# A kernel planner's transfer model: queue, engines and landing by kind, and transposes that hold the queue

## The chip, the cores and the metric

The kernel runs on one core of one Trainium2 chip. The metric is the device time of one execution in microseconds (us). Three runs of the kernel before took 1390.72 (the median), 1385.05 and 1391.09 us. The profiled execution took 1391.44 us; its instructions span 1389.6 us, and the remaining 1.84 us lie around them.

## The reference

For each of 8 sequences of 3136 rows and 256 channels, the input `x` is filtered in the frequency domain and then goes through a mixing block with a two-layer perceptron:

```python
X = np.fft.rfft(x, axis=1)
y = np.fft.irfft(X * (filt_r + 1j * filt_i), n=3136, axis=1)      # filter along the sequence
u = y + np.real(np.fft.fft(np.fft.fft(y, axis=1), axis=2))        # mix rows and channels
un = (u - mean(u)) / np.sqrt(var(u) + 1e-6)                       # over the channels
out = u + np.maximum(un @ w_ch1, 0.0) @ w_ch2                     # 256 -> 1024 -> 256
```

## The kernel before, in words

**The stages.** Each Fourier transform is split in two stages of small matrix products, with a regrouping through DRAM between them. For one sequence `b` the way is:

- `load_x` (L590) loads seven tiles of x, 480 KB each for b of 2 and over (448 KB for the first two). `measure_x` (L600) squares them on ACT, and `weigh_x` turns the result into a scale; a small PE transpose in `pow2` (L470) is its first PE step.
- `first_pair` (L671) is the first forward stage. Its results go to DRAM (`d1`, L695) and come back regrouped (`load_at`, L801).
- `spectrum` (L890) is the second forward stage. DVE (L909) and POOL (L925, L927) apply the filter, ACT and POOL (L952, L954) split the result into two fp16 halves, and a DMA transpose (L958) writes it to `z`. There are 14 of these transposes for a sequence, two for each of 7 chunks.
- `inverse1` (L1066, L1075) multiplies a chunk of `z`, and its result goes to DRAM (`d2`, L1112). `load_b2` (L1138) brings it back regrouped.
- `inverse2` (L1198) finishes the filter; `bring` (L1235) writes rows to DRAM (`dy`). `fetch` (L1264) reads them back in groups of 256.

The 8 sequences give 49 groups `g` of 256 rows, each row two tokens. `prepare` mixes channels (L1305, L1330, L1355) and normalizes; `normalize` makes `un` (L1507), splits it (L1529, L1535) and transposes it with a DMA (L1538) into `ut`; groups 0 and 6 are transposed on PE instead (L1515). `products` then runs 392 steps, eight for a group: six matmuls of the first layer (`h`, L1564), ACT and DVE split their rectified result (L1591, L1593), and twice six matmuls add the second layer (`acc`, L1604). `finish` (L1618) adds the input, and `store` (L1624) writes the result.

**What sets the order.** Every engine runs its instructions in the order in which they were emitted, and waits in place for what the next one needs. That order is made before the kernel runs, by a small planner: `Plan` (from L63 on) is an event simulation written in Python. Each stage above is a generator. It yields an engine, a length in microseconds and, if wanted, a priority; the planner lets each engine, as it comes free in planned time, take the waiting task of the lowest priority number, and only then is the task's instruction emitted. A task that needs an event (`until`), a buffer (`take`) or a step of `products` (`gate`) does not stand in line before it has come, again in planned time. The stages of a sequence are tied to the steps of `products` by such gates, so that they spread evenly among the 392 steps.

All DMAs are issued on one queue, SP's. For it the planner keeps `moved`, the planned time at which all transfers so far have been moved. A transfer that takes the queue at `now` is planned so (in `Plan.run`):

```python
issue = TURN if length == 1.65 else ISSUE
self.moved = max(self.moved, self.now + issue + REACH) + length
self.free_at[e] = max(self.now + issue, self.moved - BACKLOG)
self.end = self.moved + LANDED
```

with ISSUE 0.5, TURN 1.4, REACH 0.5, BACKLOG 4.5 and LANDED 1.5; the length 1.65 marks a DMA transpose. So the queue is taken for `issue` or until no more than 4.5 us of transfers are ahead, and the task goes on at `end`. Tasks in the line "calm" also go to SP, but only when `moved` is at most CALM (1.0) ahead.

The planner never sees the chip: where a transfer lands later than planned, an engine meets an instruction whose data are not there and waits, with everything that was emitted behind it.

Of the kernel before, what the change touches and what calls it, by code (L numbers as in the profile page):

```python
# [42 lines left out]
PASSES = ((0, 0), (1, 0), (0, 1))  # L43
BACKED = 6.5
RAW_IN = (None, None, "ys", "ys", "ut", None, None, None)
ISSUE = 0.5
TURN = 1.4
BACKLOG = 4.5
REACH = 0.5
LANDED = 1.5  # L50
HOP = 0.1
SMALL = 2.0**-20
CALM = 1.0
# [12 lines left out]
class Plan:  # L66


    def __init__(self):
        self.now = self.end = self.moved = 0.0  # L70
        self.heap, self.count, self.live = [], 0, 0
        self.queues = {e: [] for e in ("PE", "DVE", "ACT", "POOL", "SP", "calm")}
        self.free_at = dict.fromkeys(self.queues, 0.0)
# [72 lines left out]
    def given(self, ring, k):  # L146
        ring.freed.add(k)
        self.grant(ring)

    def run(self):  # L150
        while self.heap:
            self.now, _, f, args = heapq.heappop(self.heap)
            f(*args)
            while self.heap and self.heap[0][0] <= self.now:
                _, _, f, args = heapq.heappop(self.heap)
                f(*args)
            for e, queue in self.queues.items():
                if e == "calm" and queue:
                    e = "SP"
                    if self.moved > self.now + CALM:  # L160
                        self.post(self.moved - CALM, int)
                        continue
                if queue and self.free_at[e] <= self.now:
                    _, _, task, length = heapq.heappop(queue)
                    if e == "SP":
                        issue = TURN if length == 1.65 else ISSUE
                        self.moved = max(self.moved, self.now + issue + REACH) + length
                        self.free_at[e] = max(self.now + issue, self.moved - BACKLOG)
                        self.end = self.moved + LANDED
                    else:  # L170
                        self.end = self.free_at[e] = self.now + length
                    self.post(self.free_at[e], int)
                    self.step(task, None, self.free_at[e] if e == "SP" else None)
        assert not self.live
# [199 lines left out]
def _program(ctx, tc, nc, a, NB):  # L374
# [205 lines left out]
    def load_x(b, t):  # L580
        yield gate(t)
        ms[b] = tp.tile([len_of(b), 8], F32, tag="mx", name=f"mx_{b}")
        for q in range(7):
            yield gate(t + 1.2 * q)
            yield until(("own", "x", b, q))
            if b == 1:
                yield until(("asked_b2",))
            yield "calm" if b == 2 else "SP", 1.6, -62 if b == 1 else t + 1.2 * q
            src = a["x"][b] if b < WIDE else a["xq"][b - WIDE]
            nc.sync.dma_start(xs[b, q], src[:, 4 * q : 4 * q + 4])  # L590
            done("x", b, q)
# [65 lines left out]
    def first_pair(b, q, t):  # L657

        yield gate(t)
        yield until(("sx", b), ("s1q",))  # L660
        if b not in d1s:
            d1s[b] = dp.tile([2, 56, 28, 2, 256], F16, tag="d1", name=f"d1_{b}")
        x = xs[b, q]
        sx = sxs[b][:, 1:2]
        kp = yield take("psf", 2)
        ps = [bank(f"s1_{b}_{q}_{i}").rearrange("p (n c) -> p n c", n=2) for i in range(2)]
        yield "PE", FOURS, t - BOOST
        for c in range(2):
            for i in range(2):
                row = slice(64 * i, 64 * i + 56)  # L670
                nc.tensor.matmul(  # L671
                    ps[i][64 * c : 64 * c + 64], s1q[row], x[row, 2 * c : 2 * c + 2], start=True, stop=True
                )
        give("big", 21 * b + q - 7)
        kx = yield take("x16")
        odd = fp.tile([128, 2, 256], F32, tag="x16", name=f"odd_{b}_{q}", bufs=3)
        yield "ACT", 0.58
        nc.scalar.activation(odd, ps[1], AF.Copy, scale=sx)
        for out, op in ((ps[1], ALU.subtract), (odd, ALU.add)):
            yield "DVE", 0.73  # L680
            nc.vector.scalar_tensor_tensor(out, ps[0], sx, odd, op0=ALU.mult, op1=op)
        give("psf", kp)
        k = yield take("ast")
        st = fp.tile([128, 2, 2, 2, 256], F16, tag="ast", name=f"ast_{b}_{q}", bufs=3)
        yield "ACT", 0.55
        nc.scalar.copy(st[:, 1, :, 0], ps[1])
        plan.spawn(sum_half(b, q, kx, odd, st), t)
        yield "DVE", 0.66
        nc.vector.tensor_tensor(st[:, 1, :, 1], ps[1], st[:, 1, :, 0], op=ALU.subtract)
        give("psf", kp + 1)  # L690
        yield until(("sum", b, q))
        for c in range(2):
            yield "SP", 0.85
            n = 4 * q + 2 * c
            nc.sync.dma_start(  # L695
                d1s[b][:, :, n : n + 2].rearrange("s p n h c -> p s (n h c)"),
                st[64 * c : 64 * c + 56].rearrange("p s n h c -> p s (n h c)"),
            )
        give("ast", k)
        done("d1", b, 2 * q)  # L700
        done("d1", b, 2 * q + 1)
# [68 lines left out]
    turned = []  # L770
# [14 lines left out]
    def load_at(b, t):  # L785
        yield until(*(("d1", b, q) for q in range(14)))
        if b < WIDE:
            d1v = d1s[b].rearrange("(u r) n h c -> (r n h) u c", r=2)
        else:
            d1v = d1s[b].rearrange("s (j r) n h c -> (r n h) s j c", r=2)  # L790
        for ch in range(7):
            yield gate(t + max(0, ch - 2))
            yield until(("own", "at", b, ch))
            if b < WIDE:
                yield "SP", 1.95, t + max(0, ch - 2)
                nc.sync.dma_start(ats[b, ch], d1v[:, 8 * ch : 8 * ch + 8])
            else:
                at = ats[b, ch].rearrange("p (j s) c -> p s j c", s=2)
                for i in range(2):
                    yield "SP", 1.0, t + max(0, ch - 2)  # L800
                    nc.sync.dma_start(at[:, i], d1v[:, i, 4 * ch : 4 * ch + 4])  # L801
            done("at", b, ch)

# [51 lines left out]
    def spectrum(b, ch, hf, t):  # L855
# [98 lines left out]
        nc.gpsimd.tensor_tensor(y16v[:, 1], yh, y16v[:, 0], op=ALU.subtract)  # L954
        done("ylo", b, ch, hf)
        yield until(("own", "z", b, ch))
        yield "SP", 1.65
        nc.sync.dma_start_transpose(  # L958
            zs[b, ch][:, :, 128 * hf : 128 * hf + 128], y16.rearrange("p l j q -> p (l j q)")
        )  # L960
# [93 lines left out]
    def inverse1(b, ch, t):  # L1054
# [52 lines left out]
        else:  # L1107
            yield until(("low", b, ch))
        for c in range(2):
            yield "SP", 0.65  # L1110
            j = 4 * ch + 2 * c
            nc.sync.dma_start(d2s[b][:, j : j + 2], bt[64 * c : 64 * c + 56])  # L1112
        give("ast", k)
# [12 lines left out]
    def load_b2(b):  # L1126
        yield until(*((("d2", b, ch) if b else ("d2", 0, ch, h)) for ch in range(7) for h in range(1 if b else 2)))
        if b:
            d2v = d2s[b].rearrange("(i a r) j l t c -> i (r j) a (l t c)", a=2, r=2)
        else:  # L1130
            d2v = d2s[b].rearrange("(i a r) j t c -> i (r j) a (t c)", a=2, r=2)
        for c in range(7):
            yield gate(brought(b, c) - 3 - (0 if b else 3))
            k = yield take("b2")
            b2 = b2_page(k, b)
            for o in range(2):
                yield "SP", 1.0, urgent(b, c) - 3 if b or c > 1 else -63
                nc.sync.dma_start(b2[64 * o : 64 * o + 56].rearrange("p a l t c -> p a (l t c)"), d2v[2 * c + o])  # L1138
            if b == 0 and c == 1:
                plan.set(ev("asked_b2"), True)  # L1140
            b2s[b, c] = k, b2
            done("b2", b, c)
# [74 lines left out]
    def bring(b, c, o, ys, ky, kp, p):  # L1217
# [13 lines left out]
            return  # L1231
        rows = dys[b][224 * c : 224 * c + 224].rearrange("(j q) k c -> k q j c", j=4)
        for h in range(2):
            yield "SP", 0.7 - 0.17 * (c == 0)
            nc.sync.dma_start(rows[h, :, c == 0 :], ys[64 * h : 64 * h + 56, c == 0 :])  # L1235
            for kind in range(2 * (c == 0)):
                yield "SP", 0.1
                nc.sync.dma_start(
                    rows[kind, 28 * h : 28 * h + 28, 0], ys[64 * h + 28 * kind : 64 * h + 28 * kind + 28, 0]
                )  # L1240
# [7 lines left out]
    def fetch(g):  # L1248
# [7 lines left out]
        for t in range(2):  # L1256
            q, g1 = 256 * g + 128 * t, 256 * g + 128 * t + 128
            yield until(*(("placed", b, o // 2, o % 2) for b, o in pieces(q, g1, 112)))
            while q < g1:
                b = q // NS  # L1260
                e = min(g1, (b + 1) * NS)
                p = q % 128
                yield "SP", 1.6 * (e - q) / 256
                nc.sync.dma_start(y[p : p + e - q, t], dys[b][q - b * NS : e - b * NS])  # L1264
                q = e
            if t:
# [234 lines left out]
    def normalize(g, t, y, sb, ut):  # L1501
# [32 lines left out]
            yield "POOL", 1.14  # L1534
            nc.gpsimd.tensor_tensor(u16[:, :, :, 1], unv, u16[:, :, :, 0], op=ALU.subtract)  # L1535
        give("un", ku)
        yield "SP", 1.65
        nc.sync.dma_start_transpose(ut[:, t], u16.rearrange("p k d l q -> p (k d l q)"))  # L1538
        give("u16", k6)
        done("ut", g, t)  # L1540
# [79 lines left out]
        plan.spawn(store(g, t, y), 8 * g + 8)  # L1620

    def store(g, t, y):
        yield "SP", 0.8
        nc.sync.dma_start(a["out"][256 * g + 128 * t : 256 * g + 128 * t + 128], y[:, t])  # L1624
        outs[g] = outs.get(g, 0) + 1
        if outs[g] == 2:
# [250 lines left out]
```

## Time and profile before

| | |
|---|---|
| time, median of 3 runs | 1390.72 us |
| profiled execution | 1391.44 us |
| its span | 1389.6 us |
| PE busy | 1354.4 us, 97% of the span |
| DVE, ACT, POOL busy | 72%, 61%, 51% |
| mean granted TensorE clock | 0.992 of full speed |
| DMA engines, mean busy share by the queue's packets | 77.8% |
| HBM read and written | 113.72 MB and 99.09 MB |
| DMA transposes | 98 into `z`, 94 into `ut` |

PE is TensorE's matmul row. An engine that is busy 97% of the time has little idle time to lose, so the table is read together with the list of what PE waited for, and with the granted clock where PE had been idle. In the views of waits, "A <- B" is an engine's instruction and what released it. In the queue's rows, SPq is SP's queue, and the second number is how long the issue held it, not how long the transfer took.

### The profile page before, as it was taken

The page shows a single profiled execution, that of the slowest core. Times are in us where ns is not written, and L with a number is a line of the kernel's source. Part 1 is how long each engine was busy: PE and PEld are TensorE (multiplying, and loading weights), DVE is VectorE, ACT ScalarE, POOL GpSimd, SP SyncE. Part 2 cuts the span into 40 slices and gives each one's busy share as a digit, 9 for nine tenths or more (in the row PEclk, how much of TensorE's full clock was granted, in tenths as well). Part 3 has the DMA queues.
Part 4 walks back from the last instruction along what each step waited for, and adds up shares of the span by engine and source line. Part 5 has one row for each costly group of instructions (what it writes and reads, how often), then busy time and mean ns, then how long its engine had stood idle before and what let it go on. Part 6 is the DMA issues. An engine that isn't in the chain of part 4 may idle for free.

```text
span 1389.6 us, 33404 instructions
## 1 busy us (share of the span) xinstructions
PE 1354.4 (97%) x12879; PEld 917.6 (66%) x12879; DVE 997.1 (72%) x2162; ACT 845.3 (61%) x1631; POOL 706.4 (51%) x865
## 2 busy tenths in 40 slices
PE   9989999999899999999999999999899999999998
PEld 8845766666657765677656665666566776666666
DVE  6888896788678777678677875777648778465442
ACT  6776567556755677565765667647656565444341
POOL 2713881378536864388443863368614766222210
PEclk9989999999999999999999999999999999999999
DMA  9797998699889897887979797787966986554320
GB/s 259 238 249 209 240 202 208 204 227 205 195 231 238 184 199 192 256 188 185 228 197 217 174 218 182 216 205 170 221 176 180 205 197 168 141 138 105 100 61 31
DMA packets 353603, 265.35 MB, mean 191 GB/s; under 512 B 216188, under 2 KB 290588, under 8 KB 353444
## 3 DMA queue, kind: packets, MB, share of 16 engines
q1 hardware_dynamic: 353444, 263.22, 77.8%
q8 instruction: 101, 1.65, 0.5%
q14 instruction: 58, 0.48, 0.1%
HBM read 113.72 MB, written 99.09 MB: 153 GB/s over the span
## 4 chain that ended last, share of the span: by engine, by line
PE 72%; DMA 8%; DVE 7%; POOL 4%; ACT 4%; issue 3%; SPq 2%; DVEq 0%; POOLq 0%; ACTq 0%
PE acc L1604 29%; PE h L1564 29%; DMA x<-xq 4%; PE s L671 3%; PE y L1198 3%; PE s L890 2%; PE mix L1305 2%; PE i L1075 2%; DMA z<-late 1%; DMA ft<-fiT 1%; ACT xsq L600 1%; DVE h L1593 1%; DMA ft<-frT 1%; POOL eo L1011 1%; POOL late L954 1%
## 5 line engine op out<-in xcount | busy, mean ns | idle before, releaser
L1604 PE MATMUL acc<-w2s,h 128*128 128x256 f16 x4704 | 589.0, 273 | 1.2 <-ACT u L1529 1.0
L1564 PE MATMUL h<-ut,w1s 128*128 128x512 f16 x2352 | 575.6, 381 | 0.2 <-DVE ut L1521 0.2
L1604 PEld LDWEIGHTS <-h 128*128 128x128 f16 x4704 | 449.1, 98 | 138.9 <-issue 24.2
L1593 DVE SCALAR_TENSOR_TENSOR h<-h,h 128x512 f16<-128x512 f32 x392 | 267.8, 683 | 227.1 <-ACT h L1591 225.3
L1591 ACT ACTIVATE h<-h 128x512 f16<-128x512 f32 x392 | 232.8, 594 | 305.6 <-PE h L1564 303.6
L1564 PEld LDWEIGHTS <-w1s 128*128 128x128 f16 x2352 | 225.8, 98 | 205.9 <-issue 14.2
L1535 POOL TENSOR_TENSOR u<-un,u 128x512 f16<-128x512 f32 x92 | 106.4, 1157 | 222.5 <-ACT u L1529 186.5
L1355 POOL TENSOR_TENSOR pages<-sm,pages 128x508 f32<-128x508 f32 x49 | 62.0, 1266 | 107.0 <-ACT sm L1396 66.0
L1507 ACT ACTIVATE un<-pages,sb 128x256 f32<-128x256 f32 x196 | 109.0, 592 | 10.0 <-DVE sb L1454 8.9
L954 POOL TENSOR_TENSOR late<-yt,late 128x448 f16<-128x448 f32 x98 | 102.7, 1052 | 21.2 <-ACT late L952 19.8
L707 POOL TENSOR_TENSOR ast<-odd,ast 128x512 f16<-128x512 f32 x42 | 48.4, 1157 | 123.6 <-ACT ast L705 118.7
L1476 DVE BATCH_NORM_STATS2 st<-pages 128x6 f32<-128x256 f32 x196 | 80.6, 411 | 12.9 <-POOL pages L1361 11.2
L1330 DVE SCALAR_TENSOR_TENSOR pages<-mix,alpha,pages 128x254 f32<-128x254 f32 (+2 forms) x184 | 81.4, 476 | 9.0 <-ACT sm L1396 7.5
L909 DVE SCALAR_TENSOR_TENSOR yt<-s,pF,ft 128x448 f32<-128x448 f32 x98 | 66.0, 674 | 28.1 <-PE s L890 27.0
L1120 POOL TENSOR_TENSOR bt<-sd,bt 128x512 f16<-128x512 f32 x42 | 48.6, 1158 | 70.3 <-ACT bt L1118 70.0
L925 POOL TENSOR_TENSOR yt<-yt,t 128x224 f32<-128x224 f32 x98 | 64.6, 659 | 36.1 <-DVE t L909 33.7
L952 ACT CAST late<-yt 128x448 f16<-128x448 f32 x98 | 54.9, 562 | 40.0 <-POOL yt L927 39.5
L1224 ACT ACTIVATE ys<-y,alpha 128x512 f32<-128x512 f32 x98 | 62.2, 682 | 26.3 <-PE y L1198 22.3
L1618 DVE SCALAR_TENSOR_TENSOR pages<-acc,beta,pages 128x512 f32<-128x512 f32 x98 | 68.6, 741 | 7.3 <-PE acc L1604 7.2
L978 POOL TENSOR_TENSOR ef<-yt 128x224 f32<-128x224 f32 x112 | 72.6, 669 | 0.3
L1011 POOL TENSOR_TENSOR eo<-ef,eo 128x448 f16<-128x448 f32 (+6 forms) x62 | 59.7, 967 | 25.2 <-ACT eo L1007 16.9
L909 DVE SCALAR_TENSOR_TENSOR t<-s,pF,ft 128x448 f32<-128x448 f32 x98 | 65.9, 673 | 0.5 <-POOL yt L927 0.5
(191 smaller groups left out, 1676.6 us busy)
## 6 DMA issues: line engine op xcount, KB each, us to landing
pages<-d SPq DMA_DIRECT2D x112, 224.0 KB
out<-pages SPq DMA_DIRECT2D x98, 256.0 KB
pages<-dy SPq DMA_DIRECT2D x90, 256.0 KB
d<-ast SPq DMA_DIRECT2D x98, 224.0 KB
d<-bt SPq DMA_DIRECT2D x98, 224.0 KB
dy<-ys SPq DMA_DIRECT2D x96, 224.0 KB
x<-xq SPq DMA_DIRECT2D x42, 480.0 KB
at<-d SPq DMA_DIRECT2D x84, 224.0 KB
```

The costliest lines, as they stand in the source:

```text
L909: nc.vector.scalar_tensor_tensor(out, p, pF[:, 1:2], f, op0=ALU.mult, op1=ALU.mult)
L954: nc.gpsimd.tensor_tensor(y16v[:, 1], yh, y16v[:, 0], op=ALU.subtract)
L978: nc.gpsimd.tensor_tensor(eft[:, i], yt[:, 0, i], yt[:, 1, i], op=o)
L1011: nc.gpsimd.tensor_tensor(lo, efv[:, :, e0 : e0 + n], hi, op=ALU.subtract)
L1330: nc.vector.scalar_tensor_tensor(out, p, al, y, op0=ALU.mult, op1=ALU.add)
L1476: nc.vector.bn_stats(st[:, 2 * t + k], y[:, t, k])
L1507: nc.scalar.activation(un[:, k], y[:, t, k], AF.Identity, bias=sb[:, i, 1:2], scale=sb[:, i, 3:4])
L1535: nc.gpsimd.tensor_tensor(u16[:, :, :, 1], unv, u16[:, :, :, 0], op=ALU.subtract)
L1564: nc.tensor.matmul(p.rearrange("p (t k q) -> p t k q", t=2, k=2), w1s[:, d, hw, 128 * f : 128 * f + 128], utv[:, :, :, d, hx], start=i == ...
L1591: nc.scalar.activation(h[:, 0], p, AF.Relu)
L1593: nc.vector.scalar_tensor_tensor(h[:, 1], p, 0.0, h[:, 0], op0=ALU.max, op1=ALU.subtract)
L1604: nc.tensor.matmul(acc[:, kind], h[:, hh, c0 : c0 + 128], w2s[:, f, hw], start=f == 0 and kind == 0 and i == 0, stop=f == 7 and kind == 1 ...
```

## The change

It changes the planner alone. No instruction is added to the kernel or taken from it; what can change is the order on each engine's queue. The transfer rule becomes a method of its own. A transpose (length TURN, now 1.42) takes the queue for 1.3 instead of 1.4, its data start to move after 1.1 instead of 1.9, and it holds the queue until 0.3 before the transpose ahead of it has been moved. Any other transfer starts to move after 1.6 instead of 1.0, and the queue may run ahead further: 6.0 us before this transfer is counted, instead of 4.5 after it is. A transfer is planned to have landed 0.7 after it was moved, instead of 1.5.

```diff
-ISSUE = 0.5
-TURN = 1.4
+ISSUE = 0.48
+TURN = 1.42
 BACKLOG = 4.5
-REACH = 0.5
-LANDED = 1.5
+LANDED = 0.7
...
+    def transfer(self, length):
+        turned = length == TURN
+        issue, reach, room = (1.3, 1.1, BACKLOG) if turned else (ISSUE, 1.6, BACKLOG + 1.5)
+        free = max(self.now + issue, self.moved - room)
+        self.moved = max(self.moved, self.now + reach) + length
+        if turned:
+            free = max(free, self.turned - 0.3)
+            self.turned = self.moved
+        self.free_at["SP"] = free
+        self.end = self.moved + LANDED
...
                     if e == "SP":
-                        issue = TURN if length == 1.65 else ISSUE
-                        self.moved = max(self.moved, self.now + issue + REACH) + length
-                        self.free_at[e] = max(self.now + issue, self.moved - BACKLOG)
-                        self.end = self.moved + LANDED
+                        self.transfer(length)
```

The lengths of the kinds become:

| transfer | before | after |
|---|---|---|
| tile of x (L590) | 1.6 | 2.0 |
| `d1`, half a tile (L695) | 0.85 | 0.83 |
| `at` (L801), whole and half | 1.95, 1.0 | 1.75, 0.87 |
| DMA transposes (L958, L1538) | 1.65 | 1.42 |
| `d2` (L1112) | 0.65 | 0.95 |
| `b2` (L1138) | 1.0 | 0.88 |
| `dy` (L1235) | 0.7 | 0.74 |
| `fetch`, 256 rows (L1264) | 1.6 | 1.92 |
| `store` (L1624) | 0.8 | 0.61 |

## Rows read from the trace of the kernel before

**Rows 1.** The page's first part: busy time of each engine.

```profile
PE 1354.4 (97%) x12879; PEld 917.6 (66%) x12879; DVE 997.1 (72%) x2162; ACT 845.3 (61%) x1631; POOL 706.4 (51%) x865
```

**Rows 2.** Windows: stretch, its length, busy time of PE, PEld, DVE, ACT, POOL; clock; DMA.

```profile
0.00:94.00 94.00, 82.29 (x607) 69.58 (x608) 74.86 (x157) 70.16 (x145) 37.09 (x50) 0.97 0.89 249
...
140.00:1389.60 1249.60, 1226.63 (x11987) 823.33 (x11985) 885.72 (x1914) 744.03 (x1428) 658.05 (x801) 1.00 0.78 186
```

**Rows 3.** What PE waited for from 140 us on: total, times, longest.

```profile
PE i L1075 <- DMA z<-late: 7.7, 3, 6.4
PE pt_x L470 <- ACT mx L617: 6.5, 4, 2.8
...
PE acc L1604 <- ACT u L1529: 1.0, 1, 1.0
```

**Rows 4.** The queue in time, 986 to 1003 us: start, time held, line, transfer, count.

```profile
986.77 0.35 SPq L1264 DMA_DIRECT2D pages<-dy  x1
987.22 1.30 SPq L1112 DMA_DIRECT2D d<-bt  x2
988.57 2.15 SPq L590 DMA_DIRECT2D x<-xq  x3
990.82 0.41 SPq L1264 DMA_DIRECT2D pages<-dy  x1
991.27 0.71 SPq L590 DMA_DIRECT2D x<-xq  x1
992.09 3.93 SPq L958 DMA_TRANSPOSE z<-late  x1
996.13 2.15 SPq L1112 DMA_DIRECT2D d<-bt  x2
998.37 4.28 SPq L958 DMA_TRANSPOSE z<-late  x1
```

**Rows 5.** PE in time, 1000 to 1016 us; in brackets the idle time before.

```profile
1000.45 1.46 PE L1564 MATMUL h<-ut,w1s 128*128 128x512 f16 x6
1008.28 1.49 PE L1075 MATMUL i<-z,late 56*64 56x256 f16 x24 [6.38 <-DMA z<-late]
1009.71 2.74 PE L1604 MATMUL acc<-w2s,h 128*128 128x256 f16 x12
1012.25 2.17 PE L1564 MATMUL h<-ut,w1s 128*128 128x512 f16 x6
1014.25 1.47 PE L1604 MATMUL acc<-w2s,h 128*128 128x256 f16 x12
```

**Rows 6.** PE in time, 844 to 862 us.

```profile
844.95 0.85 PE L1075 MATMUL i<-z,late 56*64 56x256 f16 x24 [0.48 <-DMA z<-late]
...
856.54 0.26 PE L470 MATMUL pt_x<-ident,mx 120*1 120x120 f32 x1 [2.82 <-ACT mx L617]
856.64 2.72 PE L1604 MATMUL acc<-w2s,h 128*128 128x256 f16 x12
859.16 1.92 PE L1564 MATMUL h<-ut,w1s 128*128 128x512 f16 x6
```

**Rows 7.** Windows, columns as in rows 2, over two stretches of lower clock.

```profile
856.67:860.08 3.41, 3.41 (x16) 2.05 (x15) 1.88 (x8) 3.38 (x7) 2.04 (x2) 0.50 0.29 70
1006.85:1013.68 6.83, 5.40 (x40) 3.32 (x41) 0.87 (x3) 1.15 (x2) 1.08 (x3) 0.50 1.12 262
```

**Rows 8.** Time that an issue held the queue, by line: ns least/median/most.

```profile
L958 SPq DMA_TRANSPOSE z<-late x98: 1231/1363/6704, 149.7 to 1162.2; - x98
```

**Rows 9.** The same for an ordinary transfer of 224 KB.

```profile
L1112 SPq DMA_DIRECT2D d<-bt x98: 306/379/1508, 168.4 to 1182.7; - x98
```

**Rows 10.** The queue in time, 348 to 365 us.

```profile
348.34 4.72 SPq L590 DMA_DIRECT2D x<-xq  x6
353.17 11.35 SPq L958 DMA_TRANSPOSE z<-late  x2
```

**Rows 11.** The chain that ended last, 465 to 490 us: start, us from issue to landing.

```profile
472.94 3.10 DMA z<-late
```

More of the change, by code (lines that the diff above doesn't have):

```diff
@@ L69, in __init__ @@
     def __init__(self):
-        self.now = self.end = self.moved = 0.0
+        self.now = self.end = self.moved = self.turned = 0.0
         self.heap, self.count, self.live = [], 0, 0
@@ L587, in load_x @@
                 yield until(("asked_b2",))
-            yield "calm" if b == 2 else "SP", 1.6, -62 if b == 1 else t + 1.2 * q
+            yield "calm" if b == 2 else "SP", 2.0, -62 if b == 1 else t + 1.2 * q
             src = a["x"][b] if b < WIDE else a["xq"][b - WIDE]
@@ L692, in first_pair @@
         for c in range(2):
-            yield "SP", 0.85
+            yield "SP", 0.83
             n = 4 * q + 2 * c
@@ L794, in load_at @@
             if b < WIDE:
-                yield "SP", 1.95, t + max(0, ch - 2)
+                yield "SP", 1.75, t + max(0, ch - 2)
                 nc.sync.dma_start(ats[b, ch], d1v[:, 8 * ch : 8 * ch + 8])
@@ L799, in load_at @@
                 for i in range(2):
-                    yield "SP", 1.0, t + max(0, ch - 2)
+                    yield "SP", 0.87, t + max(0, ch - 2)
                     nc.sync.dma_start(at[:, i], d1v[:, i, 4 * ch : 4 * ch + 4])
@@ L956, in spectrum @@
         yield until(("own", "z", b, ch))
-        yield "SP", 1.65
+        yield "SP", TURN
         nc.sync.dma_start_transpose(
@@ L1109, in inverse1 @@
         for c in range(2):
-            yield "SP", 0.65
+            yield "SP", 0.95
             j = 4 * ch + 2 * c
@@ L1136, in load_b2 @@
             for o in range(2):
-                yield "SP", 1.0, urgent(b, c) - 3 if b or c > 1 else -63
+                yield "SP", 0.88, urgent(b, c) - 3 if b or c > 1 else -63
                 nc.sync.dma_start(b2[64 * o : 64 * o + 56].rearrange("p a l t c -> p a (l t c)"), d2v[2 * c + o])
@@ L1233, in bring @@
         for h in range(2):
-            yield "SP", 0.7 - 0.17 * (c == 0)
+            yield "SP", 0.74 - 0.17 * (c == 0)
             nc.sync.dma_start(rows[h, :, c == 0 :], ys[64 * h : 64 * h + 56, c == 0 :])
@@ L1262, in fetch @@
                 p = q % 128
-                yield "SP", 1.6 * (e - q) / 256
+                yield "SP", 1.92 * (e - q) / 256
                 nc.sync.dma_start(y[p : p + e - q, t], dys[b][q - b * NS : e - b * NS])
@@ L1536, in normalize @@
         give("un", ku)
-        yield "SP", 1.65
+        yield "SP", TURN
         nc.sync.dma_start_transpose(ut[:, t], u16.rearrange("p k d l q -> p (k d l q)"))
@@ L1622, in store @@
     def store(g, t, y):
-        yield "SP", 0.8
+        yield "SP", 0.61
         nc.sync.dma_start(a["out"][256 * g + 128 * t : 256 * g + 128 * t + 128], y[:, t])
```

## The prediction

> **What bounds the kernel now.** I read the busy times first. PE is busy for 1354.4 us of the span [rows 1], so the change can only win what lies between that and 1389.6 us, 35.2 us, and what PE loses at a lower clock. The windows say where the 35.2 us lie: 94 less 82.3, or 11.7 us, before products start, 23.0 us from 140 us on, the wait for the last store among them, and the small rest between [rows 2]. The waits of PE say why: from 140 us on, 7.7 us in 3 waits for transposes into `z`, 6.5 us in 4 waits of `pt_x` (the scale of a new sequence, which hangs on its last x tile through ACT), and one of 1.0 us [rows 3]. All other reasons together are small.
>
> The queue's own rows show what the two large kinds have in common. At 988.57 us x tiles are issued, four with one `fetch` between them; behind them a transpose holds the queue for 3.93 us, and after two ordinary stores the next one holds it for 4.28 us [rows 4]. PE comes to the `inverse1` that needs this second transpose and stands idle for 6.38 us, until 1008.28 [rows 5]. At 348.34 six x tiles are issued in a row, and the two transposes behind them hold the queue for 11.35 us [rows 10]. So the waits sit where x tiles and transposes meet, a few times in the run.
>
> The idle time is paid for twice. After it the granted clock is 0.50, the lower level of 1.2 GHz, for 6.83 us from 1006.85 on and for 3.41 us from 856.67 on [rows 7]. In the first, `i` takes 1.49 us where 0.85 is usual [rows 5, 6], `acc` 2.74 instead of 1.47 and `h` 2.17 instead of 1.46 [rows 5]: 0.64 + 1.27 + 0.71 = 2.6 us. In the second `acc` takes 2.72 and `h` 1.92 [rows 6]: 1.25 + 0.46 = 1.7 us.
>
> **The change part by part.** No instruction is added or removed, so PE's 1354.4 us of work stay. What moves is the order. It matters only where PE meets an instruction too early.
>
> *Transposes behind x tiles.* I put the old and the new rule, by hand, on the measured issue times from 986.77 us on [rows 4]. Old: the `fetch` is moved at 986.77 + 1.0 + 1.6 = 989.37, two `d2` at 990.67, three x tiles at 992.27, 993.87 and 995.47, `fetch` at 997.07, x at 998.67, the transpose at 1000.32, two `d2` at 1001.62, the second transpose at 1003.27; with 1.5 for landing it is there at 1004.8. PE got it at 1008.28 [rows 5], so the old plan is 3.5 us early. New: 986.77 + 1.6 + 1.92 = 990.29, then 992.19, 998.19, 1000.11, 1002.11, 1003.53, 1005.43, 1006.85, and with 0.7 it lands at 1007.55, 0.7 us early. The hold comes out right as well: the old rule holds the queue for 1.4 us at the second transpose, the new one until 1003.53 - 0.3 = 1003.23, so 4.9 us, and 4.28 us was measured [rows 4]. For the first one the new rule says until 1002.11 - 4.5 = 997.61, that is 5.5 us against 3.93.
>
> A planner that knows this gives PE other work, as products wait for nothing there: the next instructions, `acc` and `h`, run at once after the wait [rows 5]. The error falls from 3.5 to 0.7 us, by 80%; I take 75%, since the other places are not this one. What the late transposes and x tiles cost PE is 7.7 + 6.5 + 1.0 [rows 3] + 2.6 + 1.7 of lower clock = 19.5 us. Three quarters of it are a gain of 14.6 us; the ends are 19.5 (all) and half, 9.7.
>
> A transpose holds the queue for at least 1.231 us and at most 6.704 [rows 8], where an ordinary transfer holds it for 0.306 to 1.508 us [rows 9]; a hold that long only a transpose has. The Trainium skill (Advanced Engine Details and Errata, section on the X-bar transpose) says instead that transpose DMAs are as fast as regular ones. By that rule there would be no hold to plan for, and of the correction only the longer x tiles would stay, 4 x 0.4 = 1.6 of 3.5 us; the trace here does not agree.
>
> *Landings that are planned earlier.* A transpose alone was planned to land after 1.4 + 0.5 + 1.65 + 1.5 = 5.05 us, and now after 1.1 + 1.42 + 0.7 = 3.22 us; one took 3.10 us [rows 11]. So the plan is right, but 1.83 us of cover are gone, and in a full queue the landing of every kind comes 0.8 us earlier. Of 49 `inverse1` only 3 waited for `z` [rows 3], because gates hold most of them back far longer. The exposed ones are the last two chunks of the seven sequences after the first, 14 in all, as x tiles of the next sequence come among them. The two small waits for `z` were 7.7 - 6.38 = 1.32 us together, 0.66 each. From below this part costs nothing, as for the 46 without a wait; from above 14 x 0.66 = 9.2 us. I take 0.3 each, 4.2 us, between the two, since the gates cover part of them.
>
> *Other lengths.* `at`, `b2`, `d1` and stores become shorter by 0.02 to 0.20 us, `d2`, `dy` and `fetch` longer by 0.04 to 0.32. No PE wait after 140 us names `at`, so I cost them at nothing; their cover is the same gates, and without it they are of the size of the 0.66 above.
>
> *The start.* Before 94 us the new lengths reorder loads among each other. PE is idle for 11.7 us there [rows 2]; I take no change and keep 3 us, a quarter of it, both ways.
>
> **Sum**, against the profiled execution of 1391.4 us (0.7 above the median of 1390.7): 1391.4 - 14.6 + 4.2 = 1381.0 us, 0.7% under the median.
>
> **The rivals.** *The wait moves on (1387).* An x tile needs the buffer that an `inverse1` of the sequence before gives back. If that is planned later, the last x tile and `pt_x` come later too, and the 6.5 us of `pt_x` with their 1.7 us of lower clock stay in one form or another. Then the gain is three quarters of 7.7 + 1.0 + 2.6 = 11.3, so 8.5, and 1391.4 - 8.5 + 4.2 = 1387. For it speaks that the x tiles' burst itself stays, against it that products have work to put there. By the rule of the skill above it would be 46% of 19.5, 9.0 us, and about 1387 too; the trace leaves that 2 in 100. This rival, with changes that do nothing to the order at the places that matter (1391), has 0.30.
>
> *No slack left (1402).* The plan is now so tight that `inverse1` sits on PE right at the planned landing. If each of the 14 exposed ones loses the whole 1.83 us, they cost 25.6 us: 1391.4 - 14.6 + 25.6 = 1402. It decides from new waits of about 21 us on, 1.5 us each. For it speaks that a transpose's landing spreads (holds from 1.2 to 6.7 us [rows 8]), against it the 46 that wait for nothing. The Trainium skill (DMA: Bandwidth & Descriptors, section on latency and other measured facts) gives 0.2 us for an access to HBM on average and 2 us at high load, which speaks for late landings just where the plan now cuts 0.8 us; the place worked out above, among x tiles, shows the new rule 0.7 us early, so a part of that is there. Chance 0.12.
>
> **How the numbers follow.** The forecast with what surrounds it, a gain of over 0.5% (below 1383.8), has 0.58. Half a per cent is about what a measurement of this kernel can tell from no change. Within it lie the moved wait and the change without effect, 0.30; slower by more is the rival without slack, 0.12. The range: from all 19.5 us gained, no new waits and 3 us at the start, 1391.4 - 19.5 - 3 = 1369, to half of the gain, 9.2 us of new waits and 3 us lost at the start, 1391.4 - 9.7 + 9.2 + 3 = 1394. What lies outside is the rest of the slower rival and surprises at the start, together under 2 in 10.
>
> **What would show it.** Right: PE's waits for `z` and for `pt_x` from 140 us on shrink from 14.2 us to under 5, the long one of 6.38 us is gone, the clock stays at its upper level from 140 us to the end, and PE's busy time falls a little (the 4.3 us at the lower clock). The holds of the queue by transposes stay as long as they are, since only the plan of them changes. Wrong: if the waits for `pt_x` stay with the `z` waits gone, the wait has moved on; if PE waits a dozen times for 1 to 2 us for `z`, `at` or `b2`, the slack was worth more than the truth; if PE's idle time before 94 us changes by over 3 us, the start decided, which this sum leaves out.

## The result, and the profile after

The changed kernel takes 1404.2 us (median of 6 runs, 1401.2 to 1409.7) against 1390.7 (6 runs, 1385.1 to 1392.8): a ratio of 1.0115, interval 1.0093 to 1.0136. (The ratios here and below are estimated over all runs and differ a little from the quotient of the two medians, which is 1.0097 here.) It is slower, by 13.5 us. The profiled execution took 1409.7 us, the longest of the six, and its span is 1407.9; what the profiles account for below is therefore 18.3 us and not 13.5. Lines of the changed kernel from the planner's loop on are 7 higher than before: `inverse1` is L1082 for L1075, the first layer L1571 for L1564.

The page's first part after, answering to [rows 1]:

```profile
PE 1360.8 (97%) x12879; PEld 919.2 (65%) x12879; DVE 1003.0 (71%) x2162; ACT 846.7 (60%) x1631; POOL 707.7 (50%) x865
```

The same 12879 matmuls take 6.4 us longer, and the span is 18.3 us longer, so 11.9 us are new idle time. The windows, columns as in [rows 2], say where:

```profile
0.00:94.00 94.00, 81.11 (x601) 69.12 (x601) 72.04 (x151) 65.85 (x135) 37.75 (x50) 0.96 0.86 240
94.00:140.00 46.00, 40.63 (x223) 21.00 (x224) 34.07 (x88) 29.62 (x58) 6.20 (x8) 0.85 0.74 205
140.00:1407.90 1267.90, 1239.10 (x12057) 829.07 (x12055) 896.92 (x1925) 751.24 (x1439) 663.77 (x807) 0.99 0.78 184
```

Up to 140 us PE is idle for 140 - 81.11 - 40.63 = 18.3 us, where it was 140 less (1354.4 - 1226.6 = 127.8), or 12.2 [rows 1, 2]: 6.0 us more. From 140 us on it is idle for 28.8 us instead of 23.0: 5.8 us more. The three parts, 6.0 + 5.8 + 6.4, are the 18.3 us within rounding. Most of the 6.0 us lie between 94 and 140 us, where the kernel before was idle for 0.6 us:

```profile
94.00:140.00 46.00, 45.44 (x288) 24.72 (x287) 36.48 (x95) 31.07 (x59) 11.21 (x14) 0.95 0.81 220
```

Stretches at a clock of 0.50 add up to 34.1 us within the span, where they were 21.0, and 10.2 us of what is new lie before 140 us. PE's work takes about twice as long in them, so these 13 us are enough to explain the 6.4 us.

What PE waited for after, from 140 us on (total, times, longest), answering to [rows 3]:

```profile
PE h L1571 <- DMA ut<-u: 7.2, 2, 6.0
PE y L1205 <- DMA pages<-d: 3.8, 5, 1.6
PE s L897 <- DVE t L916: 3.1, 2, 2.3
PE i L1082 <- DMA z<-late: 2.2, 1, 2.2
PE pt_x L477 <- ACT mx L624: 1.6, 3, 0.8
...
PE i L1082 <- DVE bt L1112: 1.1, 1, 1.1
```

The two rows that the forecast set out to shrink did shrink: `z` from 7.7 to 2.2 us and `pt_x` from 6.5 to 1.6. Reasons that were small before have taken their place, and the first is one that the list of before doesn't have: `h`, the products themselves, waits for `ut`. The same list up to 140 us begins with the first stage of `inverse2` (`y_first`), which waited for 1.9 us before, put down to its `pages`, and now waits for 5.1, put down to an ACT instruction on raw weights (L1694):

```profile
PE y_first L1162 <- ACT cv L1694: 5.1, 1, 5.1
PE uT L1522 <- ACT un L1514: 3.8, 2, 2.4
PE pt_x L477 <- ACT mx L624: 2.6, 1, 2.6
```

PE in time around the longest wait, and behind it the windows (columns as in [rows 2]) over it and over two later places:

```profile
445.68 0.85 PE L1205 MATMUL y<-pages,i2f 56*64 56x256 f16 x24
452.54 2.74 PE L1571 MATMUL h<-ut,w1s 128*128 128x512 f16 x6 [6.01 <-DMA ut<-u]
455.08 2.19 PE L1611 MATMUL acc<-w2s,h 128*128 128x256 f16 x12
457.10 1.46 PE L1571 MATMUL h<-ut,w1s 128*128 128x512 f16 x6
```

```profile
449.70:456.50 6.80, 3.96 (x13) 1.89 (x14) 2.51 (x10) 2.58 (x6) 1.19 (x4) 0.50 0.98 252
...
954.90:958.30 3.40, 3.40 (x37) 2.65 (x33) 1.28 (x2) 1.84 (x4) 1.59 (x2) 0.50 0.67 151
1016.80:1020.20 3.40, 3.37 (x42) 2.34 (x43) 1.38 (x2) 3.40 (x8) 0.31 (x1) 1.00 1.24 332
```

This wait has the form of the one in [rows 5], 6.01 us of idle time and 6.8 us at the lower level around its end, with `h` at 2.74 instead of 1.46. Only the tile is another, and the instruction that waits is the first `h` of step 96 of products itself.

**Which transfers come late.** The start of each step of products (the first `h` of the step in PE's timeline) shows two losses. At step 8 the changed kernel is 8.9 us behind (143.2 against 134.3), from there to step 72 it neither loses nor wins (8.4 behind), and between steps 72 and 104 it falls back to 21.6 us. After that it wins 3.3 back. The queue in time shows what is late there: raw weights (`w1s`, `w2s`) and the x tiles of sequence 2. Before, first `w2s` and then the first and the last of those x tiles:

```profile
48.71 0.39 SPq L1657 DMA_DIRECT2D w2s<-w  x1
51.27 0.40 SPq L1657 DMA_DIRECT2D w2s<-w  x1
...
190.92 0.58 SPq L590 DMA_DIRECT2D x<-xq  x1
...
217.41 0.57 SPq L590 DMA_DIRECT2D x<-xq  x1
```

After:

```profile
69.30 0.39 SPq L1664 DMA_DIRECT2D w2s<-w  x1
...
90.25 0.38 SPq L1664 DMA_DIRECT2D w2s<-w  x1
...
210.44 1.29 SPq L597 DMA_DIRECT2D x<-xq  x1
...
250.96 0.42 SPq L597 DMA_DIRECT2D x<-xq  x1
```

Both kinds stand in the planner's line "calm". A calm task may go only when `moved` is at most CALM = 1.0 ahead. By the old rule a lone `d2` puts `moved` 1.0 + 0.65 = 1.65 ahead, so the line is shut for 0.65 us; by the new one 1.6 + 0.95 = 2.55 ahead, and it is shut for 1.55. The change raised the numbers that CALM is compared with and left CALM as it was.

### The profile page after: what moved, and what is told of

Its sections match the earlier page's. It is cut to its first block, busy times and chain, and to the rows that moved or that the text cites. A ratio compares the mean times of both kernels' runs of the same rounds, so it can differ in the third digit from the quotient of the medians.

```text
span 1407.9 us, 33364 instructions
## 1 busy us (share of the span) xinstructions
PE 1360.8 (97%) x12879; PEld 919.2 (65%) x12879; DVE 1003.0 (71%) x2162; ACT 846.7 (60%) x1631; POOL 707.7 (50%) x865
## 3 DMA queue, kind: packets, MB, share of 16 engines
q8 instruction: 101, 1.65, 0.5%
## 4 chain that ended last, share of the span: by engine, by line
PE 62%; DVE 7%; POOL 4%; DMA 3%; issue 3%; ACT 3%; SPq 1%; POOLq 0%; ACTq 0%; DVEq 0%
PE acc L1611 26%; PE h L1571 26%; PE s L678 3%; PE y L1205 2%; PE mix L1312 2%; PE s L897 2%; PE i L1082 1%; DVE h L1600 1%; DMA pages<-d 1%; DVE st L1483 1%; ACT un L1514 1%; POOL u L1542 1%; POOL late L961 1%; DMA x<-xq 1%; DVE sb L1455 1%
## 5 line engine op out<-in xcount | busy, mean ns | idle before, releaser
L1571 PE MATMUL h<-ut,w1s 128*128 128x512 f16 x2352 | 575.6, 381 | 7.2 <-DMA ut<-u 7.2
L1598 ACT ACTIVATE h<-h 128x512 f16<-128x512 f32 x392 | 232.8, 594 | 321.0 <-PE h L1571 317.5
L1571 PEld LDWEIGHTS <-w1s 128*128 128x128 f16 x2352 | 226.6, 98 | 211.3 <-issue 12.0
L1514 ACT ACTIVATE un<-pages,sb 128x256 f32<-128x256 f32 x196 | 109.3, 593 | 14.8 <-DVE sb L1461 12.9
L1483 DVE BATCH_NORM_STATS2 st<-pages 128x6 f32<-128x256 f32 x196 | 80.7, 412 | 12.6 <-POOL pages L1368 10.7
L1231 ACT ACTIVATE ys<-y,alpha 128x512 f32<-128x512 f32 x98 | 62.8, 685 | 22.5 <-PE y L1205 22.1
```

Of the source, the lines that this page charges most:

```text
L1483: nc.vector.bn_stats(st[:, 2 * t + k], y[:, t, k])
L1514: nc.scalar.activation(un[:, k], y[:, t, k], AF.Identity, bias=sb[:, i, 1:2], scale=sb[:, i, 3:4])
L1571: nc.tensor.matmul(p.rearrange("p (t k q) -> p t k q", t=2, k=2), w1s[:, d, hw, 128 * f : 128 * f + 128], utv[:, :, :, d, hx], start=i == ...
L1598: nc.scalar.activation(h[:, 0], p, AF.Relu)
```

## The experiments

Places are given in the same way for all kernels, each from its one profiled execution: the time at which the last of the two `w2s` and the last x tile of sequence 2 are issued, and how far steps of products start behind the kernel before (us; minus is ahead).

| kernel | last `w2s` | step 8 | last x tile | from step 72 to 104 | step 391 |
|---|---|---|---|---|---|
| before | 51.3 | 0 | 217.4 | 0 | 0 |
| after | 90.2 | +8.9 | 251.0 | +13.2 | +18.3 |
| e1 | 59.4 | +1.9 | 227.9 | +6.3 | +13.7 |
| e2 | 93.8 | +0.8 | 249.1 | +13.1 | +10.1 |
| e3 | 88.2 | +6.7 | 232.8 | +3.9 | +14.5 |
| e4 | 59.6 | +4.2 | 244.3 | +12.6 | +12.4 |
| e5 | 51.0 | -0.1 | 216.6 | -1.3 | +1.6 |
| e6 | 56.3 | +2.0 | 226.4 | +13.3 | +8.5 |
| e7 | 59.6 | +1.0 | 229.2 | -3.0 | -6.2 |
| e8 | 55.9 | -1.2 | 222.4 | +1.1 | +4.9 |
| e9 | 50.3 | -2.5 | 224.6 | -3.1 | -8.9 |
| e10 | 50.3 | -3.7 | 222.7 | +2.3 | -8.6 |
| e11 | 51.5 | -2.2 | 215.2 | -1.0 | -2.2 |
| e12 | 54.9 | +4.1 | 221.4 | +8.9 | +23.4 |
| e13 | 51.6 | +1.4 | 220.3 | +6.2 | +16.0 |
| e14 | 88.1 | +4.2 | 232.0 | +8.4 | +10.8 |
| e15 | 66.9 | +4.4 | 249.3 | +22.5 | +24.4 |
| e16 | 90.2 | +9.2 | 259.5 | +14.1 | +8.7 |

**The calm line.** The first theory: the calm line is what makes the kernel slower. Four kernels: the changed one with the line opened again (e1), the kernel before with CALM lowered by the 0.6 us by which the new rule starts ordinary transfers later (e2), and two that open it in the changed kernel for one kind alone, by a second line that opens at 1.6: the x tiles of sequence 2 (e3), or weights and tables (e4).

```diff
-CALM = 1.0
+CALM = 1.6        # e1, from the changed kernel
...
-CALM = 1.0
+CALM = 0.4        # e2, from the kernel before
...
-            yield "calm" if b == 2 else "SP", 2.0, -62 if b == 1 else t + 1.2 * q
+            yield "quiet" if b == 2 else "SP", 2.0, -62 if b == 1 else t + 1.2 * q    # e3
...
-            yield "calm", 1.9
+            yield "quiet", 1.9    # e4, raw weights; the tables in the same way
```

> The changed kernel with CALM 1.6 in place of 1.0: the calm line opens again as soon after another transfer as it did before, when a transfer began to move 1.0 after its issue and not 1.6. Theory A (the calm line starves): the last x tile of sequence 2, issued at 217 us before and at 251 us after the change, comes before 235 us, the wait of PE for ut of 6.0 us near 452 us is gone, and the 13 us lost between steps 80 and 104 come back: about 1388 us (1380 to 1394). Theory B (the earlier planned landings leave no slack): no change, 1400 us or more.

> The kernel before with CALM 0.4 in place of 1.0, so that its calm line is as tight as in the changed kernel, and nothing else. Theory A: sequence 2's last x tile moves from 217 us to later than 235 us and the kernel becomes slower by 8 to 18 us, 1399 to 1409 us. Theory B: its landings are planned as before, so it stays within 4 us of 1391.

> The changed kernel with a second calm line, which opens at 1.6, for the x tiles of sequence 2 alone; weights and tables stay in the line that opens at 1.0. Theory A, if sequence 2 is the whole loss after the start: the 13 us between steps 80 and 104 come back, the 8 us at the start stay: about 1391 us. If the weights matter as well it stays above e1. Theory B: 1400 us or more.

> The other half: the second calm line is for the raw weights and the tables, and the x tiles of sequence 2 stay in the tight one. Theory A, if late weights are what delays the start: step 8 of the products, at 134.3 us before and 143.2 us after the change, comes back to 137 us or earlier, and the loss between steps 80 and 104 stays: about 1398 us. If the start is late for the longer x tiles of its own, step 8 stays near 143 us and the time near 1404. Theory B: 1400 us or more.

Measured: e1 1402.0 us, ratio 1.0101 (1.0062 to 1.0141); e2 1399.9, 1.0112 (1.0066 to 1.0157); e3 1405.2, 1.0134 (1.0104 to 1.0163); e4 1403.8, 1.0112 (1.0069 to 1.0155).

By their times, e1, e3 and e4 came out as theory B expected (1400 us or more) and e2 as theory A did. e2 shows that a shut calm line alone is enough to lose about as much as the whole change does. Its last x tile goes out at 249.1 us and it loses 13.1 us between steps 72 and 104, as the changed kernel does; PE's waits from 140 us on name `z` there, the longest 9.8 us:

```profile
PE i L1075 <- DMA z<-late: 18.0, 5, 9.8
```

e3 and e4 show that each kind causes its own loss in the changed kernel. With the x tiles let through, the loss from step 72 to 104 falls from 13.2 to 3.9 us; with the weights let through, step 8 is 4.2 instead of 8.9 us behind, and the wait for `ut` stays:

```profile
PE h L1572 <- DMA ut<-u: 5.9, 1, 5.9
```

Late weights do not cost that in every order: in e2 the last `w2s` goes out at 93.8 us, and step 8 is only 0.8 us behind. The wait of `h` at step 96 goes with the x tiles. Of the changed kernel and its variants, those whose last x tile of sequence 2 goes out at 244.3 us or later wait there for 5.0 to 7.4 us (after, e4, e15, e16), and those in which it goes out at 232.8 us or earlier for at most 1.6 us (e1, e3, e8, e10, e14).

But the time didn't follow. e1 lets both through, mends the places (+1.9 and +6.3), and is not measurably faster than the changed kernel: its PE waits elsewhere instead. Its list from 140 us on begins:

```profile
PE y L1205 <- DMA pages<-d: 5.0, 8, 1.5
PE i L1082 <- DMA z<-late: 4.2, 2, 2.7
PE i L1082 <- DMA d<-bt: 3.9, 1, 3.9
PE pt_x L477 <- ACT mx L624: 2.8, 1, 2.8
```

So the calm line is one cause, and there is at least one more that stands behind it. Nor are late x tiles the only way to lose between steps 72 and 104: e6, below, loses 13.3 us there with the last x tile at 226.4, and e12 8.9 us with it at 221.4.

**The other parts one by one, from the kernel before.** The hold alone (e5), the earlier landing alone (e6), and the new lengths of the ordinary transfers alone (e7).

```diff
+                        if length == 1.65:    # e5
+                            self.free_at[e] = max(self.free_at[e], self.turned - 0.3)
+                            self.turned = self.moved
...
-LANDED = 1.5
+LANDED = 0.7    # e6
...
-            yield "calm" if b == 2 else "SP", 1.6, -62 if b == 1 else t + 1.2 * q
+            yield "calm" if b == 2 else "SP", 2.0, -62 if b == 1 else t + 1.2 * q    # e7, and the other lengths of the table
```

> The kernel before with the hold alone: a transpose holds the planned queue until 0.3 us before the transpose ahead of it has been moved; every length and landing stays. Theory A (the mechanism of the forecast): the waits where x tiles and transposes meet shrink, 6.4 us at 1002 us above all, and the kernel becomes faster by 5 to 12 us. Theory C (what counts is the cover between planned and measured landing, and the hold moves only the second transpose of a pair): within 4 us of the kernel before.

> The kernel before with LANDED 0.7 in place of 1.5 alone, so that everything is planned to land 0.8 us earlier. Theory C (cover): more and longer waits of PE after 140 us, by 4 to 12 us, and a slower kernel, 1393 to 1401 us. Theory A: the gates cover it, within 4 us of the kernel before.

> The kernel before with the new lengths of all ordinary transfers and nothing else; transposes keep 1.65. Theory A: longer x tiles push inverse1 behind the products, the waits for z and pt_x shrink, and the kernel is faster by 3 to 10 us. Theory D (longer x tiles at the very start delay the weights in the calm line, and those of sequence 2 close it): the first step of the products, at 93.6 us before, comes 2 to 5 us later, and the kernel is slower by 3 to 12 us.

Measured: e5 1388.7 us, 0.9999 (0.9975 to 1.0023); e6 1398.0, 1.0075 (1.0050 to 1.0100); e7 1385.0, 0.9974 (0.9956 to 0.9992). The first row on `z` in PE's waits from 140 us on, of e5, e6 and e7:

```profile
PE i L1078 <- DMA z<-late: 10.7, 7, 3.2
```

```profile
PE i L1075 <- DMA z<-late: 10.9, 3, 6.1
```

```profile
PE i L1075 <- DMA z<-late: 3.5, 2, 2.8
```

The hold, on which the forecast built, gains nothing: from 140 us on no wait of PE is longer than 3.2 us any more and none of `pt_x` is left, but the waits for `z` grow from 3 to 7 and from 7.7 to 10.7 us. The new lengths (x tiles, `d2`, `dy` and `fetch` longer; `at`, `b2`, `d1` and stores shorter; not parted here) halve the waits for `z` and gain 0.3%; all but the x tiles the forecast costed at nothing. Landings planned earlier make the waits for `z` longer, 10.9 us, and cost 0.75%.

**x tiles of the first sequence, and what is left.** In e7 products begin 4.2 us later, though its last step is 6.2 us ahead: x of sequence 0 is loaded before anything else can run, and the planner now takes 2.0 us for each tile there too. e8 is e1 with 1.6 for them, e9 is e7 with 1.6. e10 is e8 with LANDED back at 1.5. e11 is a control: the kernel before with a later start of ordinary transfers, 1.6 instead of 1.0, and CALM moved along with it.

```diff
-            yield "calm" if b == 2 else "SP", 2.0, -62 if b == 1 else t + 1.2 * q
+            yield "calm" if b == 2 else "SP", 1.6 if b == 0 else 2.0, -62 if b == 1 else t + 1.2 * q    # e8, e9, e10
...
-LANDED = 0.7
+LANDED = 1.5    # e10
...
-CALM = 1.0
+CALM = 1.6    # e11
...
-                        self.moved = max(self.moved, self.now + issue + REACH) + length
+                        self.moved = max(self.moved, self.now + (1.9 if length == 1.65 else 1.6)) + length    # e11
```

> e1 with the x tiles of the first sequence planned at 1.6 again. Theory D: the start comes back, step 0 within 2 us of 93.6 and step 8 within 2 us of 134.3, where e1 was 4.2 and 1.9 us late, and the kernel gains 2 to 4 us on e1: about 1398. Theory C: the waits after 140 us stay at some 25 us, so the kernel stays above 1394.

> e7 (the kernel before with the new lengths) with the x tiles of the first sequence at 1.6 again. Theory D: the start, 4.2 us late at step 0 in e7, comes back to within 1 us of 93.6 and the gain of e7 grows by 2 to 4 us: about 1382 us, 0.5% faster than before. If e7's gain hung on its own late start, no more than e7: 1385 or above.

> e8 with LANDED 1.5 in place of 0.7, so that of the change only CALM and the first x tiles (mended) and the landing are undone. Theory C (cover): the waits of PE after 140 us fall from 20 us to under 14 us, and the kernel gains 5 to 10 us on e8: 1386 to 1392 us. If the cover is not it: 1395 or above.

> The kernel before with ordinary transfers planned to start moving 1.6 after their issue and CALM moved along to 1.6, nothing else. Theory C: 0.6 us more cover for ordinary transfers, so no more waits than before, within 5 us of the kernel before or faster. If the later reach itself costs: 1394 us or more.

Measured: e8 1396.8 us, 1.0055 (1.0033 to 1.0077); e9 1381.9, 0.9948 (0.9929 to 0.9967); e10 1384.6, 0.9968 (0.9951 to 0.9985); e11 1389.8, 1.0014 (1.0000 to 1.0027).

The wait of `y_first` goes with the x tiles of the first sequence: it is 5.9 us in e7, 6.5 in e1 and 6.6 in e4, where the weights are let through, and 2.1 and 2.3 us in e8 and e9, where these tiles are planned at 1.6 again. They are not all of it: in e15, below, they are planned at 2.0, and it is 2.4 us.

e11 says that the later start of ordinary transfers costs nothing that can be told, as long as CALM moves with it. From e1 over e8 to e10 the changed kernel gets 5.2 (the intervals of these two overlap) and then another 12.2 us faster, and ends below the kernel before with the hold, the earlier transposes and all new lengths but that of the first x tiles still in it. So three edits together (CALM, the first x tiles, the landing) undo the loss. e9, which takes of the change only the lengths, again without the first x tiles, has the lowest time of all, 6 us below the kernel before; its interval and that of e10 overlap. Its windows, columns as in [rows 2]:

```profile
0.00:94.00 94.00, 82.04 (x608) 69.51 (x609) 75.56 (x157) 71.20 (x147) 37.13 (x50) 0.95 0.88 250
140.00:1380.70 1240.70, 1223.42 (x11970) 821.11 (x11968) 882.94 (x1911) 745.62 (x1427) 658.55 (x801) 1.00 0.79 187
```

From 140 us on PE is idle for 17.3 us, against 23.0 [rows 2] and 28.8 after.

**The transposes.** e12 is the kernel before with the transposes' new timing and nothing else; e13 adds the hold to it; e14 takes the hold out of the changed kernel; e16 gives the transposes their old timing back in the changed kernel.

```diff
-TURN = 1.4
+TURN = 1.3    # e12, e13
...
-                        self.moved = max(self.moved, self.now + issue + REACH) + length
+                        self.moved = max(self.moved, self.now + (1.1 if length == 1.65 else 1.0)) + length - 0.23 * (length == 1.65)    # e12, e13
...
-            free = max(free, self.turned - 0.3)    # e14
...
-        issue, reach, room = (1.3, 1.1, BACKLOG) if turned else (ISSUE, 1.6, BACKLOG + 1.5)
+        issue, reach, room = (1.4, 1.9, BACKLOG) if turned else (ISSUE, 1.6, BACKLOG + 1.5)    # e16
...
-        self.moved = max(self.moved, self.now + reach) + length
+        self.moved = max(self.moved, self.now + reach) + length + 0.23 * turned    # e16
```

> The kernel before with the new timing of a transpose alone: taken for 1.3, moving after 1.1, length 1.42, without the hold; alone it is planned to land after 4.02 instead of 5.05 us. Theory C: one more us of cover lost on transposes, more waits of PE for z, slower by 2 to 8 us. If gates cover the transposes (the forecast's reading): within 3 us of the kernel before.

> The kernel before with the transposes' new timing and the hold together. The timing alone gave 1.0204, the hold alone 0.9999. Theory 'the hold pays for the earlier transposes': together at most 1.010 (1402 us or less), with half of the 34.8 us of PE idle time after 140 us gone. Rival 'the parts add up' (the hold does nothing here either): 1.017 to 1.024.

> The changed kernel without the hold. Theory 'the hold pays for the earlier transposes': 10 us or more above the changed kernel, 1.018 or more of the kernel before. Rival (the hold does nothing): 1.008 to 1.015, as the changed kernel.

> The changed kernel with the transposes' own timing back (queue 1.4, start after 1.9, 1.65 long), the hold and all else as changed. Theory 'any cover given back to the transposes pays': 6 to 12 us below the changed kernel. Rival 'other transfers' landings matter, not the transposes': within 4 us of it.

Measured: e12 1416.1 us, 1.0204 (1.0179 to 1.0230); e13 1404.8, 1.0132 (1.0104 to 1.0160); e14 1404.8, 1.0138 (1.0106 to 1.0170); e16 1398.6, 1.0055 (1.0041 to 1.0069).

Transposes that are planned 1.0 us earlier cost 2.0%, the most of any single part. PE's waits from 140 us on, of e12 and of e13:

```profile
PE i L1075 <- DMA z<-late: 17.3, 4, 8.5
PE i L1075 <- DMA x<-xq: 4.7, 1, 4.7
```

```profile
PE i L1078 <- DMA z<-late: 23.0, 5, 8.4
```

The hold takes about a third of the loss back, 0.7 of 2.0%, which is neither of the two outcomes expected; and not by shorter waits for `z`, which grow from 17.3 to 23.0 us. In the changed kernel it makes no difference to the time (e14), though without it PE waits for `z` for 10.5 us in all instead of 2.2; the longest of these waits, 6.3 us, is at step 74, and at the place of [rows 5] e14 waits for 2.1 us, as the changed kernel does (2.2):

```profile
PE i L1081 <- DMA z<-late: 8.4, 2, 6.3
...
PE i L1072 <- DMA z<-late: 2.1, 2, 1.1
```

The old timing of the transposes takes 5.6 us off the changed kernel (e16), just short of the 6 expected, though its calm line is still shut: the last x tile goes out at 259.5 us, and its `h` still waits 5.0 us for `ut`.

**Landing back in the changed kernel itself.** e15 is the changed kernel with LANDED at 1.5 and nothing else.

```diff
-LANDED = 0.7
+LANDED = 1.5
```

> The changed kernel with LANDED back at 1.5, all else as changed. Giving it back on top of the mended calm line and x tiles gained 12 us. Theory 'the cover removed costs apart from the start': 8 to 14 us below the changed kernel here too, 1390 to 1396 us, ratio 1.001 to 1.005, with PE's idle time after 140 us down from 25 to under 19 us. Rival 'the calm line decides': within 4 us of the changed kernel.

Measured: 1415.8 us, 1.0182 (1.0157 to 1.0206). That is 11.6 us slower than the changed kernel, where 8 to 14 faster was expected. Its calm line is shut too, the last x tile at 249.3 us, the loss from step 72 to 104 is 22.5 us, and its list of waits from 140 us on begins with the same wait as the changed kernel's:

```profile
PE h L1571 <- DMA ut<-u: 11.9, 3, 7.4
PE s L897 <- DVE sd L1097: 4.0, 1, 4.0
```

So "0.8 us of cover on every landing are worth some 10 us" is not a rule. It holds from the kernel before (e6 loses 10) and with the calm line mended (e10 wins 12), and turns round in e15, where the calm line is shut; why it does so there, no run shows. e10 and e15 differ only in CALM and in x of sequence 0: 1.0182 against 0.9968, about 30 us at the same LANDED; at LANDED 0.7 the same two edits are worth about 7 us (e8 against the changed kernel).

## Why the prediction was wrong

The forecast was 1381.0 us with a range of 1369 to 1394; 1404.2 came. The rival "No slack left (1402)", which had 0.12, is near in number, but that is luck: its 14 `inverse1` that lose 1.83 us each for `z` did not come, the changed kernel has one such wait of 2.2 us from 140 us on. Waits for `z` of nearly that size in all came in other kernels (e2 18.0 us, e12 17.3, e13 23.0).

- *What bounds the kernel* was read rightly. The change wins or loses through PE's idle time and the lower clock around it: in the profiles 11.9 us of new idle time and 6.4 us of slower work on PE make up the 18.3 us.
- *"Transposes behind x tiles"*: the waits forecast to go went, but the hold is not what pays. `z` and `pt_x` fell from 14.2 us [rows 3] to 3.8, under the 5 asked for, the 6.38 us [rows 5] shrank to one wait of 2.18, and no `pt_x` waits as in [rows 6] from 140 us on. Counted by steps, the changed kernel wins 4.6 us from step 216 to 224 and 6.9 from step 256 to 272, 11.5 together and near the 14.6 forecast. But the hold alone gains nothing (e5), and the clock didn't stay at its upper level. What gained alone were the new lengths (e7, e9). The working by hand says so too when it is taken apart: between the old and the new rule the second transpose is moved 3.58 us later, by four x tiles 1.6, four `d2` 1.2, two `fetch` 0.64 and the later start 0.6, less 0.46 for two shorter transposes; the hold is in none of it. So the sentence that without the hold only the 1.6 us of the x tiles would stay is wrong, and so is the 46% that the first rival takes from it. And "the trace here does not agree", said of the holds in [rows 8] and [rows 9], goes further than these rows: they give how long an issue held the queue, not how fast a transpose's data move.
- *"Landings that are planned earlier"* is the term of the sum that was mis-sized: 4.2 us, bounded by 9.2. Alone, the transposes' part is +28 us (e12, 2.0% of 1388) and the common 0.8 us is +10 (e6, 0.75%). It was sized by 14 exposed `inverse1` at 0.3 us. In e12 PE is idle for 38.5 us from 140 us on instead of 23.0, and 22.0 of them, against 7.7 for `z` before, are in 4 waits for `z` of up to 8.5 us and one of 4.7 us for x: not many small waits but a few long ones. The bound of 0.66 us for each, the size of the small waits seen before, had no ground, since the gates that covered the 46 others act in the same planned time that was moved. Nor is the price fixed: giving the transposes their old timing back in the changed kernel wins 5.6 us and not 28 (e16), and e10 has the earlier transposes in it and is below the kernel before.
- *The missing step* is the calm line. The description of the kernel says that its tasks go only when `moved` is at most 1.0 ahead; the change adds to `moved` for every ordinary transfer, and no sentence of the prediction puts the two together. e2 shows its price alone, 1.1% (0.7 to 1.6).
- *"The start"* was taken as no change with 3 us both ways. The changed kernel is 8.9 us behind by step 8. Two edits meet there: x tiles of sequence 0 planned longer (e7 begins products 4.2 us later, e9 0.7 us earlier) and weights held up in the calm line (e4 takes 4.7 of the 8.9 us back). The sign that the prediction named did not show it: before 94 us PE's idle time changes by 1.2 us only, from 11.7 to 12.9. It grows behind that, between 94 and 140 us, from 0.6 to 5.4 us with the clock at 0.85 instead of 0.95, a stretch that the sum passes over as "the small rest".
- *The rival "The wait moves on"* had the right thought, that a late x tile holds up what hangs on it, and the wrong tile: not the last ones of each sequence through `pt_x`, but sequence 2's through the calm line, and by way of its stores and `fetch` to `ut` of group 12, 200 us later. That chain is read from issue times in the traces; the runs show that late x tiles go with the wait at step 96 and bring the loss there (e2, e3), not each link.

The parts do not add up. Hold 0, transposes +2.0%, landing +0.75%, shut calm line +1.1% (e2), lengths -0.3% make +3.6%, and the change costs 1.15%. The new limit on how far the queue may run ahead and ISSUE 0.48 were not run alone; e10 has both in it. Every edit gives another order from its first place on, and a part's price depends on which waits the rest of that order has left. The intervals cover repeats of one order, not the choice of it: no run shows how far the time moves under an edit that ought to mean nothing, so of a single part's price some may be the luck of its order. e11 shows how much can move at the same time: `z` falls from 7.7 to 4.4 us and `pt_x` from 6.5 to 2.3, and one wait of 6.5 us of `uT` for `un` takes their place. So what is shown is where the changed kernel loses and which three edits together undo it (e10); what each part costs by itself, and which later waits e1 and e15 got from which transfer, stays open.

## What to carry to other kernels

Where an order is made from a cost model, making one of its numbers truer can take away slack that another number had lent: of this change's parts, planning landings earlier cost time alone (e6, e12), planning the hold did nothing (e5), and only the lengths gained. Look for every constant that is compared with the one that changes, and move it along; CALM against the start of a transfer was worth 1.1% alone (e2), though moving it along did not win that back by itself (e1). And try the parts one by one before the whole: here the version with the lowest time, e9 at 0.9948, is one part of the change with an exception for the first load.

## What the runs showed that was not expected

The clock does not follow the length of a wait alone. In the changed kernel PE's clock falls to 0.50 for the 3.40 us from 954.90 on, after two waits of 1.63 and 0.47 us for pages of `inverse2` within 2.4 us; after the single wait of 2.18 us that ends at 1016.83 it stays at 1.00 (the windows at 954.90 and 1016.80 above):

```profile
953.01 0.30 PE L1205 MATMUL y<-pages,i2f 56*64 56x256 f16 x2 [1.63 <-DMA pages<-d]
953.77 0.84 PE L1205 MATMUL y<-pages,i2f 56*64 56x256 f16 x22 [0.47 <-DMA pages<-d]
...
1016.83 0.85 PE L1082 MATMUL i<-z,late 56*64 56x256 f16 x24 [2.18 <-DMA z<-late]
```

So two short waits in a row cost more there than one longer one. Nor does the lower level begin behind a long wait, as the prediction has it: in [rows 5] and [rows 7] it begins at 1006.85, 1.4 us before the wait ends, and in the changed kernel it holds from 449.70 on, in a wait that ends at 452.54. That part of it costs nothing.

A transpose holds the queue behind x tiles in the changed order as well. The row on all 98 transposes into `z`, answering to [rows 8], and the queue in time where the changed kernel issues four x tiles:

```profile
L965 SPq DMA_TRANSPOSE z<-late x98: 1231/1296/5584, 157.7 to 1173.2; - x98
```

```profile
1003.05 2.57 SPq L597 DMA_DIRECT2D x<-xq  x4
1005.73 0.47 SPq L1119 DMA_DIRECT2D d<-bt  x1
1006.29 5.54 SPq L965 DMA_TRANSPOSE z<-late  x1
```

The longest hold is 5.58 us instead of 6.70 and the median 1.30 instead of 1.36. Holds of over 2 us are 24 before and 21 after among these 98, and 16 and 19 among the 94 transposes into `ut`. The plan that knows of holds avoids few of them; it only no longer counts on the time.
